# Interleaving upper-weight and lower-weight matmul passes, and moving the upper weights in SBUF, in a windowed-attention and SoLU kernel

## The chip, the cores and the metric

The kernel runs on one core of a Trainium2 chip. The metric is device time in microseconds, from the start to the end of one execution. Before the change three runs took 518.44, 518.72 and 519.62 us; their median is 518.72.

## What is computed

Attention with a causal window of 64 keys over 8 sequences of 576 tokens with 8 heads of 64, and behind it a gated projection block on the 4608 resulting rows of 512:

```python
scores = scale * np.matmul(q, k.transpose(0, 1, 3, 2))
mask = (rel >= 0) & (rel < window)
attn = softmax(np.where(mask, scores, -1e9))
x = np.matmul(attn, v)                      # rows of 512
h = x @ w_in                                # 512 -> 1024
solu = h * softmax(h)
ln = (solu - mean(solu)) / np.sqrt(var(solu) + 1e-06) * g_ln
out = ln @ w_out                            # 1024 -> 512
```

All of it is in float32, and most of the multiplications belong to the two projections.

## The kernel before, in words

The 4608 rows are 36 tiles of 128. For each tile there are scores, a softmax, a transposition of its weights, the products with v, the input projection (`moe_in`), the SoLU and its normalisation, another transposition, and the output projection (`moe_out`). The tiles are staggered: while tile t is in `moe_in`, tile t - 2 is in `moe_out`.

**The passes.** TensorE runs a float32 matmul at half rate, in two instructions. So from input tile 3 (`PLAIN_IN`) and output tile 2 (`PLAIN_OUT`) on, each operand is held as an upper part, rounded to the float32r format, and a lower part, the remainder in the same format; upper times upper, upper times lower and lower times upper are added up in PSUM. One such product of a 128x128 stationary operand and a 128x512 moving one is called a pass here. The stationary operand is a column block of x or y (`xH`, `xL`, `yH`, `yL`), the moving one a row of weights of 512 float32r values, 2048 bytes in each partition: `WH`, the upper weights, in the two const tiles `w_inH` and `w_outH`, or `WL`, the lower weights, in tiles of the ring `w`. `split` (line 384) makes both from the weights that `weight_block` decoded, with the normalisation's gain `g_sb` multiplied into the output's.

A tile's input projection has 24 passes (L601): for each of four blocks c of x, two halves d of 512 columns, and three products. The halves lie in two PSUM banks (`pH`). A tile's output projection also has 24 (L735): eight blocks f of y and three products, taken in pairs f, f + 1, all into one bank (`pO`). In both, one loop writes out six passes at a time, in the order of the list `passes` (lines 594 and 730): upper x with upper weights twice, lower x with upper weights twice, upper x with lower weights twice. Input tile 3 alone is done in two halves, its passes sorted so that all with upper weights come first (line 597). In the last tiles `moe_out` places the transposition of the next tile's halves between its passes (`middle`, line 732).

**The order.** `Plan` collects every operation with its engine, a planner's cost (a pass: 235) and what it reads and writes. TensorE's operations keep the order in which the program names them; the other engines' are placed by due times that follow from TensorE's order, with hand-set offsets (`HINTS`). SyncE's queue issues all DMAs.

**The places.** Tiles of the pool `const` come first in SBUF, in the order of their making, each padded to a multiple of 32 bytes in a partition; then the rings. Between `w_inH` and the ring of q and k lie 2 x 16384 bytes of weights, 32 of `g_sb` and 32 for `neghalf`; the ring of q and k has 3 x 5120, and every ring behind it that a pass reads starts a multiple of 2048 bytes further on. By 2048 bytes, `w_inH` and `w_outH` begin at a rest of 896, and `w`, `xH`, `xL`, `yH` and `yL` at 1984 (896 + 64 + 15360 = 7 x 2048 + 1984). Each slice of weights that a pass reads is 2048 bytes long and has its tile's rest; the blocks of x and y are 512 bytes apart.

Of the kernel before, what the change touches and what calls it, by code (L numbers as in the profile page):

```python
# [9 lines left out]
F32 = mybir.dt.float32  # L10
# [9 lines left out]
P = 128  # L20
# [206 lines left out]
def tile_window_attention_solu_moe(  # L227
# [25 lines left out]
    NC = DM // P  # L253
    NF = DFF // P
# [4 lines left out]
    const = ctx.enter_context(tc.tile_pool(name="const", bufs=1))  # L259
# [20 lines left out]
    for first in (0, None, 1):  # L280
# [3 lines left out]
        if first is not None:  # L284
            nc.gpsimd.memset(t[first * WIN:(first + 1) * WIN, :WIN], NEG)

    w_inH = const.tile([P, NC, DFF], F32R, name="w_inH")
    w_outH = const.tile([P, NF, DM], F32R, name="w_outH")
    g_sb = const.tile([P, NF], F32, name="g_sb")
    neghalf = const.tile([P, 1], F32, name="neghalf")  # L290
    nc.gpsimd.memset(neghalf, -0.5)

# [2 lines left out]
    def T(tag, n, shape, dtype=F32, pool=None):  # L295

        if (tag, n) not in plan.tiles:
            plan.tiles[tag, n] = (pool or sb).tile(
                shape, dtype, tag=tag, name=f"{tag}_{n}", bufs=RINGS[tag])
        return plan.tiles[tag, n]  # L300
# [8 lines left out]
    def W32(i):  # L309
        return T("w", i, [P, 2, 512])  # L310

    def WL(i):
        return T("w", NW + i, [P, 2, 512], F32R)

    def WH(i, x):
        if i < NC:
            return w_inH[:, i, x * 512:(x + 1) * 512]
        return w_outH[:, 2 * (i - NC) + x]
# [121 lines left out]
    def PE_T(t, x):  # L440
        return PS(NTILE + t)[:, x]
# [102 lines left out]
    def XH(t):  # L544
        return T("xH", t, [P, NC, P], F32 if t < PLAIN_IN else F32R)
# [31 lines left out]
    def PH(t):  # L577
        return T("pH", t, [P, DFF], pool=ps_h)

    def E(t):  # L580
        return T("e", t, [P, DFF])

    def moe_in(t, h):
        if t < PLAIN_IN:

            for c in range(NC if h == 0 else 0):
                for x in range(2):
                    plan.op("PE", 860, lambda c=c, x=x: nc.tensor.matmul(  # L588
                        PH(t)[:, x * 512:(x + 1) * 512], XH(t)[:, c], W32(c)[:, x],
                        start=(c == 0), stop=(c == NC - 1)),  # L590
                        [("xH", t, c // 2), ("w", c), ("w", c, x)], [("pH", t)])
            return
        kinds = (XH, WH, "xH", "H", 0), (XH, WL, "xH", "w", NW), (XL, WH, "xL", "H", 0)
        passes = [(c, d, *kinds[k]) for c in range(NC) for d, k in ((0, 0), (1, 0), (0, 2), (1, 2), (0, 1), (1, 1))]
        if t == PLAIN_IN:

            passes = sorted((p for p in passes if p[1] == h), key=lambda p: p[5] == "w")
        elif not h:
            passes = []
        for n, (c, d, x, w, xk, wk, o) in enumerate(passes):  # L600
            plan.op("PE", 235, lambda n=n, c=c, d=d, x=x, w=w: nc.tensor.matmul(  # L601
                PH(t)[:, d * 512:(d + 1) * 512], x(t)[:, c], WH(c, d) if w is WH else WL(c)[:, d],
                start=all(p[1] != d for p in passes[:n]), stop=all(p[1] != d for p in passes[n + 1:])),
                [(xk, t), (wk, o + c, d)], [("pH", t)])
# [37 lines left out]
    def YH(t):  # L642
        return T("yH", t, [P, NF, P], F32 if t < PLAIN_OUT else F32R)

    def YL(t):
        return T("yL", t, [P, NF, P], F32R)

    def crosses(t):
        return CROSS_FROM <= t < NTILE - CROSS_END
# [21 lines left out]
    def moe_join(t):  # L671
        def Y(h):
            return T("y", t, [P, NF, P])[:, 4 * h:4 * h + 4]

        for h in range(2):
            hs = slice(4 * h, 4 * h + 4)
            plan.op("DVE", 740, lambda h=h: nc.vector.tensor_copy(
                Y(h).bitcast(U16).rearrange("p f (n w) -> p f w n", w=2),
                TP(t, h).rearrange("p w f n -> p f w n")),
                [("raw", NW + 2 * t + 1, 2 + h)], [("y", t, h)], port=True)  # L680
            plan.op("ACT", 620, lambda h=h, hs=hs: nc.scalar.copy(YH(t)[:, hs], Y(h)),
                    [("y", t, h)], [("yH", t, h)])
            plan.op("DVE", 690, lambda h=h, hs=hs: nc.vector.tensor_sub(
                YL(t)[:, hs], Y(h), YH(t)[:, hs].bitcast(F32)),
                [("y", t, h), ("yH", t, h)], [("yL", t, h)], port=True)

    def moe_transpose(t, halves=range(2)):
        if crosses(t):
            moe_join(t)
            return  # L690
        for h in halves:
            def pT(h=h):
                return PE_T(t, h)

            def emit(h=h, pT=pT):
                for f in range(4):
                    c = 4 * h + f
                    nc.tensor.transpose(pT()[:, f], E(t)[:, c * P:(c + 1) * P], ident)  # L698

            hs = slice(4 * h, 4 * h + 4)  # L700
            plan.op("PE", 430, emit, [("e", t, h)], [("pS", NTILE + t, h)])
            if t < PLAIN_OUT:
                plan.op("DVE", 690, lambda hs=hs, pT=pT: nc.vector.tensor_tensor(
                    YH(t)[:, hs], pT(), g_sb[:, hs].unsqueeze(2).to_broadcast([P, 4, P]), op=ALU.mult),
                    [("pS", NTILE + t, h), ("g",)], [("yH", t, h)])
                continue
            plan.op("ACT", 560, lambda hs=hs, pT=pT: nc.scalar.copy(YH(t)[:, hs], pT()),  # L707
                    [("pS", NTILE + t, h)], [("yH", t, h)])
            plan.op("DVE", 690, lambda hs=hs, pT=pT: nc.vector.tensor_sub(  # L709
                YL(t)[:, hs], pT(), YH(t)[:, hs].bitcast(F32)),  # L710
                [("pS", NTILE + t, h), ("yH", t, h)], [("yL", t, h)])

    def moe_out(t, middle=None):

        tag = ("pO", t)

        def PO():
            return T(*tag, [P, DM], pool=ps_o)

        if t < PLAIN_OUT:  # L720
            for f in range(NF):
                plan.op("PE", 860, lambda f=f: nc.tensor.matmul(  # L722
                    PO(), YH(t)[:, f], W32(NC + f // 2)[:, f % 2],
                    start=(f == 0), stop=(f == NF - 1)),
                    [("yH", t, f // 4), ("w", NC + f // 2), ("w", NC + f // 2, f % 2)], [tag])
        kinds = (
            (YH, lambda i, x: WH(i, x), "yH", "H", 0),
            (YH, lambda i, x: WL(i)[:, x], "yH", "w", NW),
            (YL, lambda i, x: WH(i, x), "yL", "H", 0))
        passes = [(f + d, *kinds[k]) for f in range(0, NF, 2) for d, k in ((0, 0), (1, 0), (0, 2), (1, 2), (0, 1), (1, 1))]  # L730
        for n, (f, y, w, yk, wk, o) in enumerate(passes if t >= PLAIN_OUT else []):
            if n in (NF // 2 * 3, NF // 4 * 9) and middle is not None:
                moe_transpose(middle, (f // 2 % 2,))
            i, x = NC + f // 2, f % 2
            plan.op("PE", 235, lambda n=n, f=f, i=i, x=x, y=y, w=w: nc.tensor.matmul(  # L735
                PO(), y(t)[:, f], w(i, x), start=(n == 0), stop=(n == len(passes) - 1)),
                [(yk, t, f // 4), (wk, o + i, x)], [tag])

        def ot():
            return T("ot", t, [P, DM])  # L740

        if t == NTILE - 1:
            for x, copy in enumerate((nc.scalar.copy, nc.vector.tensor_copy)):
                xs = slice(x * DM // 2, (x + 1) * DM // 2)
                plan.op("DVE" if x else "ACT", 360, lambda xs=xs, copy=copy: copy(ot()[:, xs], PO()[:, xs]),
                        [tag], [("ot", t, x)])
                plan.dma(P * DM * 2, lambda xs=xs: nc.sync.dma_start(out[t * P:(t + 1) * P, xs], ot()[:, xs]),
                         [("ot", t, x)], [], True)
            return
        plan.op("ACT", 580, lambda: nc.scalar.copy(ot(), PO()), [tag], [("ot", t)])  # L750
        plan.dma(P * DM * 4, lambda: nc.sync.dma_start(out[t * P:(t + 1) * P, :], ot()), [("ot", t)], [],
                 t > SPL, 420)
# [49 lines left out]
    for t in range(NTILE + BEHIND):  # L802
# [6 lines left out]
        if t == PLAIN_IN:  # L809
            for i in range(NC):  # L810
                split(i)
        on(moe_in, t, 0)
        if t == 0:
            scores(2)
            softmax(2)
        if t < BEHIND:
            on(moe_in, t, 1)
            on(moe_norm, t)
            on(moe_cross, t)
# [78 lines left out]
```

## Time and profile before

| | |
|---|---|
| median of three runs | 518.72 us |
| the profiled execution | 518.59 us |
| its span, first to last instruction | 516.7 us |
| TensorE busy | 497.0 us, 96% |
| VectorE busy | 409.2 us, 79% |
| ScalarE busy | 355.3 us, 69% |
| GpSimd busy | 315.2 us, 61% |
| mean granted clock of TensorE | 1.00 |

The profile is of one execution. Its times are in microseconds unless marked ns; PE is TensorE's matmuls, PEld its weight loads, DVE VectorE, ACT ScalarE, POOL GpSimd, and L601 is line 601 of the kernel. Matmuls overlap their successors, so the length of one row is longer than the distance between two starts, and the pace is read from the starts.

### The profile page before, as it was taken

The numbers are of one execution on the slowest core, as the hardware profiler recorded it, in microseconds if no ns is written. First come the engines' busy times: TensorE is split into PE (matmuls) and PEld (weight loads), VectorE is DVE, ScalarE is ACT, GpSimd is POOL, SyncE is SP. The second block draws the span as 40 slices with busy tenths as digits, with TensorE's granted clock in tenths as the row PEclk, the third lists the DMA queues.
The fourth block names the chain that finished last, engine by engine and source line by source line (L and its number), as shares of the span: only waits on it lengthen the run. The fifth ranks groups of instructions, "written<-read, shape, count | busy, mean of one in ns | idle before, by whom it ended". The sixth has DMA issues, their size and how long they took to land.

```text
span 516.7 us, 11600 instructions
## 1 busy us (share of the span) xinstructions
PE 497.0 (96%) x4064; PEld 391.7 (76%) x4064; DVE 409.2 (79%) x1176; ACT 355.3 (69%) x960; POOL 315.2 (61%) x566
## 2 busy tenths in 40 slices
PE   2789999999999999999999999999999999999997
PEld 1445567888888888787888888888888888888875
DVE  5998997878887879796978798877888878877531
ACT  4589795867686858586867777675858585855331
POOL 4388566665757575747474857484747476945430
PEclk9999999999999999999999999999999999999999
DMA  8994455977999989878888897879797968654301
GB/s 322 412 410 161 122 119 127 217 159 153 209 185 173 202 203 185 200 186 187 198 167 212 162 226 165 225 151 236 127 253 145 246 120 224 124 123 102 82 20 43
DMA packets 150762, 94.09 MB, mean 182 GB/s; under 512 B 135088, under 2 KB 135344, under 8 KB 150320
## 3 DMA queue, kind: packets, MB, share of 16 engines
q1 hardware_dynamic: 150704, 93.35, 75.6%
q8 instruction: 32, 0.52, 0.5%
q14 instruction: 26, 0.21, 0.1%
HBM read 50.86 MB, written 9.44 MB: 117 GB/s over the span
## 4 chain that ended last, share of the span: by engine, by line
PE 89%; POOL 2%; ACT 1%; DVE 1%; issue 0%; ACTq 0%
PE pO L735 37%; PE pH L601 35%; PE pO L557 7%; PE pS L458 6%; PE pO L722 3%; PE pH L588 1%; POOL sS L496 1%; PE pS L698 1%; ACT sS L478 0%; POOL mst L624 0%; DVE w L391 0%; DVE yL L709 0%; POOL raw L358 0%; ACT sq L627 0%; ACT yH L707 0%; DVE e L621 0%
## 5 line engine op out<-in xcount | busy, mean ns | idle before, releaser
L496 POOL TENSOR_SCALAR sS<-sS,rec 128x128 f32<-128x128 f32 x280 | 147.9, 550 | 11.7 <-PE pS L458 7.4
L478 ACT ACTIVATE sS<-sS,nmx 128x128 f32<-128x128 f32 x288 | 111.5, 389 | 1.5 <-DVE nmx L473 1.4
L735 PE MATMUL pO<-w_outH,yH 128*128 128x512 f32 x272 | 86.9, 400 | 0.0
L735 PE MATMUL pO<-w_outH,yL 128*128 128x512 f32 x272 | 85.4, 394 | 0.0
L735 PE MATMUL pO<-w,yH 128*128 128x512 f32 x272 | 84.8, 393 | 0.0
L601 PE MATMUL pH<-w_inH,xL 128*128 128x512 f32 x264 | 83.5, 394 | 0.0
L601 PE MATMUL pH<-w_inH,xH 128*128 128x512 f32 x264 | 83.5, 395 | 0.0
L601 PE MATMUL pH<-w,xH 128*128 128x512 f32 x264 | 81.9, 393 | 0.0
L510 ACT COPY raw<-sS 128x1024 uint16<-128x1024 uint16 x64 | 66.7, 1046 | 20.9 <-POOL sS L496 20.9
L630 POOL TENSOR_SCALAR mst<-mst 128x1 f32<-128x1 f32 x36 | 21.4, 593 | 79.4 <-ACT sq L627 42.8
L638 POOL TENSOR_SCALAR e<-e,mst 128x512 f32<-128x512 f32 x72 | 66.8, 938 | 3.8
L571 ACT CAST xH<-pO 128x512 fp32r<-128x512 f32 x33 | 19.4, 586 | 71.1 <-PE pO L557 71.1
L616 DVE TENSOR_REDUCE mst<-pH 128x1 f32<-128x1024 f32 x36 | 44.0, 1222 | 30.2 <-PE pH L601 30.1
L520 DVE COPY PT<-raw 128x1024 uint16<-128x1024 uint16 x64 | 50.2, 792 | 19.9 <-DMA raw<-raw 19.6
L735 PEld LDWEIGHTS pO<-w,yH 128*128 128x128 f32 x272 | 50.9, 187 | 12.4
L735 PEld LDWEIGHTS pO<-w_outH,yL 128*128 128x128 f32 x272 | 51.1, 188 | 11.7
L624 POOL TENSOR_SCALAR mst<-mst 128x1 f32<-128x1 f32 x36 | 18.8, 523 | 66.7 <-DVE mst L621 60.7
L735 PEld LDWEIGHTS pO<-w_outH,yH 128*128 128x128 f32 x272 | 49.5, 188 | 12.7 <-issue 2.6
L601 PEld LDWEIGHTS pH<-w_inH,xH 128*128 128x128 f32 x264 | 49.6, 188 | 12.0 <-DVE mst L625 0.2
L601 PEld LDWEIGHTS pH<-w,xH 128*128 128x128 f32 x264 | 49.4, 187 | 12.0
L601 PEld LDWEIGHTS pH<-w_inH,xL 128*128 128x128 f32 x264 | 49.6, 188 | 11.3 <-issue 0.2
L627 ACT ACTIVATE sq<-e,mst 128x1024 bf16<-128x1024 f32 x36 | 41.4, 1150 | 20.0 <-POOL mst L624 20.0
(71 smaller groups left out, 850.3 us busy)
## 6 DMA issues: line engine op xcount, KB each, us to landing
qk<-qk SPq DMA_DIRECT2D x36, 640.0 KB, 5.9
v<-vS SPq DMA_DIRECT2D x36, 512.0 KB, 4.6
y<-ot SPq DMA_DIRECT2D x35, 256.0 KB, 2.5
raw<-w_out SPq DMA_DIRECT2D x4, 1024.0 KB, 11.9
raw<-w_in SPq DMA_DIRECT2D x3, 1024.0 KB, 11.7
raw<-raw SPq DMA_TRANSPOSE x126, 3.2
raw<-w_in SPq DMA_DIRECT2D x2, 512.0 KB, 6.2
y<-ot SPq DMA_DIRECT2D x2, 128.0 KB, 1.7
```

The lines of the kernel that those rows point to most:

```text
L458: nc.tensor.matmul(PS(t, p // 2)[half * WIN:(half + 1) * WIN, r, p], q[rs, p, half * WIN:(half + 1) * WIN], keys, start=True, stop=True)
L478: plan.op("ACT", 390, lambda h=h: nc.scalar.activation(SS(t)[:, h], SS(t)[:, h], AF.Exp, bias=cols("nmx", h), scale=-1.0, accum_out=cols(" ...
L496: plan.op(engine, cost, lambda h=h: v.tensor_scalar(SS(t)[:, h], SS(t)[:, h], rec()[:, h:h + 1], 0.0, ALU.mult, ALU.add), [R], [("sS", t, ...
L510: plan.op("ACT", 1050, lambda x=x: nc.scalar.copy(XP(t)[:, x], SS(t)[:, 4 * x:4 * x + 4].bitcast(U16).rearrange("p h (n w) -> p w (h n)", ...
L520: plan.op("DVE", 740, lambda x=x: nc.vector.tensor_copy(PT(t)[:, 4 * x:4 * x + 4].bitcast(U16).rearrange("p h (n w) -> p h w n", w=2), XP( ...
L557: nc.tensor.matmul(PX(t, p)[r * D:(r + 1) * D, p, ks], V(t, half)[:, h * D:(h + 1) * D], PT(t)[:, h, ks], start=True, stop=True)
L601: plan.op("PE", 235, lambda n=n, c=c, d=d, x=x, w=w: nc.tensor.matmul(PH(t)[:, d * 512:(d + 1) * 512], x(t)[:, c], WH(c, d) if w is WH els ...
L616: plan.op("DVE", 1225, lambda: nc.vector.tensor_reduce(nmax(), PH(t), axis=AX.X, op=ALU.max, negate=True), [("pH", t)], [key(0)])
L627: plan.op("ACT", 1150, lambda: nc.scalar.activation(T("sq", t, [P, DFF], BF16), E(t), AF.Square, bias=nmean(), scale=1.0, accum_out=ss()), ...
L630: plan.op("POOL", 240, lambda: nc.gpsimd.tensor_scalar(kk(), ss(), se(), se(), ALU.mult, ALU.mult), [key(1), key(3)], [key(5)])
L638: plan.op("POOL", 770, lambda h=h, hs=hs: nc.gpsimd.tensor_scalar(E(t)[:, hs], E(t)[:, hs], nmean(), kk(), ALU.add, ALU.mult), [key(4), ke ...
L735: plan.op("PE", 235, lambda n=n, f=f, i=i, x=x, y=y, w=w: nc.tensor.matmul(PO(), y(t)[:, f], w(i, x), start=(n == 0), stop=(n == len(passe ...
```

## The change

The list of six passes gets another order in both projections: upper x with upper weights and then with lower weights, the same for the second half (or block), and then lower x with upper weights twice. Two const tiles that nothing reads or writes are put in, of 272 x 4 = 1088 bytes ahead of `w_inH` and of 240 x 4 = 960 behind `g_sb`. The upper weights and `g_sb` so begin 1088 bytes later, at a rest of 1984 by 2048 bytes, and all that follows begins 2048 bytes later, at the rest that it had. The block that `middle` transposes is found from n instead of f, since f runs in another order.

```diff
+    const.tile([P, 272], F32, name="shift")
     w_inH = const.tile([P, NC, DFF], F32R, name="w_inH")
     w_outH = const.tile([P, NF, DM], F32R, name="w_outH")
     g_sb = const.tile([P, NF], F32, name="g_sb")
+    const.tile([P, 240], F32, name="gap")
     neghalf = const.tile([P, 1], F32, name="neghalf")
...
         kinds = (XH, WH, "xH", "H", 0), (XH, WL, "xH", "w", NW), (XL, WH, "xL", "H", 0)
-        passes = [(c, d, *kinds[k]) for c in range(NC) for d, k in ((0, 0), (1, 0), (0, 2), (1, 2), (0, 1), (1, 1))]
+        passes = [(c, d, *kinds[k]) for c in range(NC) for d, k in ((0, 0), (0, 1), (1, 0), (1, 1), (0, 2), (1, 2))]
...
-        passes = [(f + d, *kinds[k]) for f in range(0, NF, 2) for d, k in ((0, 0), (1, 0), (0, 2), (1, 2), (0, 1), (1, 1))]
+        passes = [(f + d, *kinds[k]) for f in range(0, NF, 2) for d, k in ((0, 0), (0, 1), (1, 0), (1, 1), (0, 2), (1, 2))]
         for n, (f, y, w, yk, wk, o) in enumerate(passes if t >= PLAIN_OUT else []):
             if n in (NF // 2 * 3, NF // 4 * 9) and middle is not None:
-                moe_transpose(middle, (f // 2 % 2,))
+                moe_transpose(middle, (n // 6 % 2,))
```

## Rows read from the trace of the kernel before

**Rows 1.** The page: busy time, share and count; the chain's shares by line.
```profile
PE 497.0 (96%) x4064; PEld 391.7 (76%) x4064; DVE 409.2 (79%) x1176; ACT 355.3 (69%) x960; POOL 315.2 (61%) x566
...
PE pO L735 37%; PE pH L601 35%; PE pO L557 7%; PE pS L458 6%; PE pO L722 3%; PE pH L588 1%; POOL sS L496 1%; PE pS L698 1%; ACT sS L478 0%; POOL mst L624 0%; DVE w L391 0%; DVE yL L709 0%; POOL raw L358 0%; ACT sq L627 0%; ACT yH L707 0%; DVE e L621 0%
```

**Rows 2.** The page's costliest groups: two of the six groups of passes.
```profile
L735 PE MATMUL pO<-w_outH,yH 128*128 128x512 f32 x272 | 86.9, 400 | 0.0
...
L601 PE MATMUL pH<-w_inH,xL 128*128 128x512 f32 x264 | 83.5, 394 | 0.0
```

**Rows 3.** Waits of TensorE, the first of eight: us in total, times, longest.
```profile
PE pS L531 <- DVE sS L496: 4.9, 1, 4.9
...
```

**Rows 4.** 100 to 480 us: busy PE, PEld, DVE, ACT, POOL (counts), granted clock, DMA share, GB/s.
```profile
100.00:480.00 380.00, 380.00 (x3185) 311.51 (x3184) 310.32 (x894) 270.41 (x728) 246.18 (x433) 1.00 0.83 181
```

**Rows 5.** The longest wait of any engine in the same stretch.
```profile
ACT xH L571 <- PE pO L557: 64.2, 15, 4.9
...
```

**Rows 6.** The chain in order of time: start, us, what.
```profile
202.53 5.55 PE pH L601 x24
208.07 5.55 PE pO L735 x24
```

**Rows 7.** Timeline of TensorE, input tile 13: start, us, pass, count.
```profile
202.36 0.62 PE L601 MATMUL pH<-w_inH,xH 128*128 128x512 f32 x2
202.82 0.63 PE L601 MATMUL pH<-w_inH,xL 128*128 128x512 f32 x2
203.29 0.62 PE L601 MATMUL pH<-w,xH 128*128 128x512 f32 x2
203.75 0.62 PE L601 MATMUL pH<-w_inH,xH 128*128 128x512 f32 x2
204.21 0.63 PE L601 MATMUL pH<-w_inH,xL 128*128 128x512 f32 x2
204.68 0.62 PE L601 MATMUL pH<-w,xH 128*128 128x512 f32 x2
205.14 0.62 PE L601 MATMUL pH<-w_inH,xH 128*128 128x512 f32 x2
205.59 0.63 PE L601 MATMUL pH<-w_inH,xL 128*128 128x512 f32 x2
206.06 0.62 PE L601 MATMUL pH<-w,xH 128*128 128x512 f32 x2
206.52 0.62 PE L601 MATMUL pH<-w_inH,xH 128*128 128x512 f32 x2
206.98 0.63 PE L601 MATMUL pH<-w_inH,xL 128*128 128x512 f32 x2
207.45 0.62 PE L601 MATMUL pH<-w,xH 128*128 128x512 f32 x2
207.91 0.39 PE L735 MATMUL pO<-w_outH,yH 128*128 128x512 f32 x1
```

**Rows 8.** The view of the tile w_outH: first pass, last writing of the lower weights.
```profile
L735 PE MATMUL pO<-w_outH,yH x272: 391/392/502, 90.1 to 511.7; 128*128 128x512 f32 x136
...
L397 DVE SCALAR_TENSOR_TENSOR w<-w,g_sb,w_outH x8: 699/742/848, 68.3 to 83.0; 128x512 fp32r<-128x512 f32 x8
```

**Rows 9.** Timeline of TensorE, input tile 3: ends of its runs.
```profile
64.51 0.40 PE L601 MATMUL pH<-w_inH,xL 128*128 128x512 f32 x1
...
66.15 1.09 PE L601 MATMUL pH<-w,xH 128*128 128x512 f32 x4
67.08 0.39 PE L601 MATMUL pH<-w_inH,xH 128*128 128x512 f32 x1
...
68.94 1.08 PE L601 MATMUL pH<-w,xH 128*128 128x512 f32 x4
69.86 0.38 PE L698 MATMUL pS<-ident,e 128*128 128x128 f32 x2
```

**Rows 10.** The chain in order of time: an output tile in fp32.
```profile
73.01 7.06 PE pO L722 x16
```

## Prediction, made before the change was timed

> **What bounds the kernel now.** I read the page first. TensorE is busy for 497.0 us of a span of 516.7, 96%, and the lines of the two projections, L735 and L601, have 37% and 35% of the chain that ended last [rows 1]. The groups of the page say what these are: six groups of 264 or 272 matmuls of 128x512, together 3 x 264 + 3 x 272 = 1608 passes [rows 2]. Then the waits. Of TensorE's own there are eight kinds; the longest is 4.9 us, at a transposition of the start, and none is at the lines of the passes [rows 3]. In the stretch from 100 to 480 us TensorE is busy for all 380 us, at a granted clock of 1.00 (the upper of its two levels, 2.4 GHz), while VectorE has 310 us of work, ScalarE 270 and GpSimd 246 [rows 4]; the longest wait there is ScalarE's, 64.2 us, and it is for TensorE [rows 5]. So the end is set by how fast the passes follow one another, and little else.
>
> How fast they do is seen in the chain in order of time: a tile's 24 passes are one piece of 5.55 us in either projection [rows 6]. 5.55 us / 24 = 231.25 ns a pass. That is the number that this change can move: 1608 passes x 1 ns = 1.6 us, 0.3% of the whole.
>
> The pace is not one number, and the timeline of TensorE by passes shows it [rows 7]. It merges each pair of the old order. The start of a pair to the start of the next, summed over the four sixes of tile 13: upper weights with the upper x, 0.46 + 0.46 + 0.45 + 0.46 = 1.83 us for eight passes, 228.8 ns each; upper weights with the lower x, 4 x 0.47 = 1.88 us, 235 ns; lower weights, 4 x 0.46 = 1.84 us, 230 ns (each sum good to about 0.01 us, so 1 ns a pass). The moving operands of the first two pairs have the same addresses, the loads are equally large, and nothing waits. So more than its addresses decides how long a pass takes: what came before it has a part.
>
> **The change, part by part.** No instruction comes or goes. Two const tiles are reserved and never written; they shift addresses only. The edit in `moe_transpose`'s argument picks the same halves: at n = 12 the old form gives f = 4, 4 // 2 % 2 = 0, the new 12 // 6 % 2 = 0, and at n = 18 both give 1. It costs nothing. Tile 3's input passes are sorted, and come out in the old order.
>
> *The order and the other engines.* The lower x and the lower y are wanted two passes later in each six, the lower weights three (or two) passes earlier, some 0.5 to 0.7 us. All have cover: TensorE never waits at a pass, so neither lower x nor lower y is late today, and both are wanted later still [rows 3]; the lower output weights' last writing begins at 83.0 us and lasts at most 0.85, while the first pass that reads upper output weights starts at 90.1 [rows 8]. Without that cover the loss would be those 0.7 us, once. The queues are untouched: no DMA is added, and none is moved in the program; the planner may place a VectorE or ScalarE operation differently, which costs nothing while TensorE waits for nobody. A faster TensorE would need the others to follow: at 310 us of 380 VectorE has a margin of 18%, and the change can ask 1 or 2% of it.
>
> *The order and TensorE.* A pass takes its stationary operand new each time already, as many weight loads as matmuls [rows 1], so that one x now serves four passes in a row saves no load. Both projections take 5.55 us for 24 passes, though the input's alternates between two PSUM banks and the output's stays in one [rows 6]; the new order of banks (0 0 1 1 0 1) should cost nothing.
>
> *The addresses.* Upper weights begin at a rest of 896 by 2048 bytes now, everything else that a pass reads (lower weights, x and y, upper and lower) at 1984. The new place gives all of them 1984. Nothing in the trace has all operands at one rest in a long run, so this term is bounded by the nearest rows. Unfavourable end: what passes do that read one rest without a break. Tile 3 has such runs of upper weights, seven passes from 64.51 to 66.15 us and eight from 67.08 to 68.94 [rows 9]: 1.64 + 1.86 = 3.50 us for 15, 233.3 ns; the slowest pair is 235. Favourable end: the fastest pair, 228.8 ns; and since that is an average over a pair in a pattern that was not made for it, I let the low end go as far below it again as it lies below the mean, 226.3 ns. Further out, the half-rate passes of the fp32 tiles (16 in 7.06 us [rows 10], 441 ns) say that a full-rate pass without any excess would take at most half, 221 ns; nothing speaks for going there.
>
> I take the fastest pair. Reasons: the four lower-weight passes that close tile 3 (0.92 us, 230 ns) and tile 13's lower pairs (230) read everything at 1984 and are under the mean, though a change of rest comes right before or behind them; and the slow pairs, 235, are those where upper weights at 896 have settled. Sum: (228.8 - 231.25) x 1608 = -3.9 us. The profiled execution took 518.59 us (its span 516.7 and 1.9 around it), 0.13 less than the median of 518.72; so 514.7.
>
> **The rivals.**
>
> *It settles slow (slower).* The mechanism: the length of a pass depends on how the read of the moving operand falls against the load of the next stationary one, and runs of one rest lock into the long position, as tile 3's 15 passes with upper weights did at 233.3 ns [rows 9]. Today the jump from 896 to 1984 and the one back, in every six passes, break that lock, and make the 228.8 that follow them; with one rest no jump is left. Price: (233.3 - 231.25) x 1608 = +3.3 us, 522.0; at the 235 of the slowest pair +6.0. It decides if the mean of the new passes is over 231.9 ns. For it: it is the only long run in the trace whose moving operands share one rest. Against it: that run's stationary operands had another rest than its moving one, as the new passes don't have.
>
> *Addresses change nothing (same).* TensorE reads both operands, and if the two reads don't hinder each other, or if only the mean counts, one order is as good as another: tile 3's eight lower-weight passes took 0.93 + 0.92 = 1.85 us, 231.3 ns, with all at 1984 [rows 9], exactly today's mean. Then 518.6 to 518.8. The Trainium skill speaks for this one (TensorE: Matmul & The Clock Gate, Part 2): the moving operand and the weight load have SBUF read ports of their own, and loading the next weights takes nothing from the running matmul. By that rule no shift of addresses could pay. The trace disagrees in part: equal passes differ by 228.8 to 235 ns [rows 7].
>
> *The change doesn't do what it says.* If rests by 2048 are not what counts, only the order is left: four changes between upper and lower weights in six passes instead of two. This falls into one of the two cases above, and has no chance of its own.
>
> **How the numbers follow.** A measurement of this kernel can tell about 0.2%, 1.0 us or 0.65 ns a pass, from no change. Forecast 0.50 (nearly all of it faster), slow settling 0.30, nothing changes 0.20. That gives faster 0.49, same 0.20, slower 0.31. The range: below, 226.3 ns, -8.0 us, 510.7; above, the slow settling at 522.0 and some 0.4 for a schedule that the planner makes worse, 522.4. About 1 in 10 is left out on either side, 235 ns for all passes above, and anything near 221 ns below. Signs are mixed, so the forecast's own range: 510.7 to 517.5.
>
> **What would show it.** Right: pieces of 24 passes at 5.49 us or less instead of 5.55, with TensorE busy throughout from 100 to 480 us still. Tile 3 keeps its order, so its 15 passes with upper weights show the address by itself: under 233 ns if one rest is the better one. Settling slow shows as pieces of 5.60. If the pieces are shorter and the total is not, waits of TensorE at L601 or L735 appear, on a VectorE subtraction or a DMA. Wrong altogether: pieces of 5.55 us as before, or pairs that differ as before though every operand has one rest.

## The result, and the profile after

The changed kernel takes 512.75 us (median of four runs, 511.89 to 513.02), the kernel before beside it 518.64 (518.44 to 519.62): ratio 0.9879, interval 0.9866 to 0.9891, 5.9 us or 1.2% faster. The forecast was 514.7: right side, inside its range, and 2 us too timid. The profiled execution took 513.01 us, with a span of 510.9. Lines behind the two new tiles have moved by two: L601 and L735 are L603 and L737 now.

The page after, busy time and the chain's shares, answers to [rows 1]:

```profile
PE 492.1 (96%) x4064; PEld 392.4 (77%) x4064; DVE 409.8 (80%) x1176; ACT 355.6 (70%) x960; POOL 314.5 (62%) x566
...
PE pH L603 34%; PE pO L737 34%; PE pO L559 6%; PE pS L460 6%; PE pO L724 3%; PE pH L590 1%; DMA raw<-raw 1%; ACT sS L480 1%; POOL sS L498 1%; PE pS L700 1%; DVE e L623 1%; DVE mst L618 1%; DMA y<-ot 1%; ACT e L620 0%; DVE w L368 0%
```

As many instructions as before on every engine, TensorE still at 96%, and the two projections still the chain, now with 34% each instead of 35 and 37. New among the chain's shares are a few per cent of other engines; they lie ahead of one late wait, read below.

The chain in order of time (start, us, what), for [rows 6]:

```profile
195.87 5.67 PE pO L737 x24
201.54 5.44 PE pH L603 x24
206.98 5.44 PE pO L737 x24
```

A tile's piece went from 5.55 to 5.44 us, 226.7 ns a pass, in both projections. The 5.67 is a tile that follows attention; before, these took 5.76.

TensorE's timeline of the same input tile 13 as in [rows 7], start, duration, pass, count:

```profile
201.38 0.39 PE L603 MATMUL pH<-w_inH,xH 128*128 128x512 f32 x1
201.60 0.39 PE L603 MATMUL pH<-w,xH 128*128 128x512 f32 x1
201.83 0.39 PE L603 MATMUL pH<-w_inH,xH 128*128 128x512 f32 x1
...
202.74 0.39 PE L603 MATMUL pH<-w_inH,xH 128*128 128x512 f32 x1
...
206.81 0.39 PE L737 MATMUL pO<-w_outH,yH 128*128 128x512 f32 x1
```

Read starts, not durations (0.39 us overlaps the next pass). Start to start it is 0.22 or 0.23 throughout, six passes from 201.38 to 202.74 make 1.36 us, and 24 make 5.43 (5.440 by the trace's starts in ns). The unequal pairs of before are gone: upper and lower, x and weights, all pace alike.

Tile 3, whose order the change leaves alone, in the timeline after, for [rows 9]:

```profile
64.14 0.39 PE L603 MATMUL pH<-w_inH,xL 128*128 128x512 f32 x1
...
65.75 1.08 PE L603 MATMUL pH<-w,xH 128*128 128x512 f32 x4
66.67 0.39 PE L603 MATMUL pH<-w_inH,xH 128*128 128x512 f32 x1
...
68.48 1.07 PE L603 MATMUL pH<-w,xH 128*128 128x512 f32 x4
69.39 0.60 PE L700 MATMUL pS<-ident,e 128*128 128x128 f32 x4
```

Its 15 passes with upper weights take 1.61 + 1.81 = 3.42 us where they took 3.50: 228.0 ns instead of 233.3, the last eight 226 to 227. Here nothing but the address of the weights has changed.

Of the waits of TensorE after, for [rows 3], the one that is new (us in total, times, longest), and the stretch from 100 to 480 us, for [rows 4]:

```profile
PE pH L603 <- DVE mst L623: 0.8, 1, 0.8
```

```profile
100.00:480.00 380.00, 379.23 (x3233) 315.34 (x3232) 315.51 (x899) 271.54 (x728) 246.03 (x432) 1.00 0.84 182
```

48 more of TensorE's instructions (3233 for 3185) fit into the same 380 us, at the same granted clock of 1.00. VectorE has 315.5 us of work in it instead of 310.3. And TensorE is no longer busy for all of it: 0.77 us are idle, one wait at a pass (L603), where before there was none.

**Where the time went.** I compared the start of each of the 67 tiles in the two timelines. Of a tile that follows another without a break, 46 in all, the step to the next start is 0.107 us shorter; of the 19 that begin behind attention or other work it is about 0.094, since their first passes don't pace yet (below), and of the two with a transposition between their passes 0.055. That makes 46 x 0.107 + 19 x 0.094 + 2 x 0.055 = 6.8 us. In the trace the lead over the kernel before grows from 0.38 us at tile 3 to 1.14 at output tile 5, and falls to 0.32 at input tile 8, where the wait is: against the step that was due, 0.93 us go in the wait and 0.08 at the tile's first pass, and the others run at 227 ns at once. Another 0.27 us goes at input tile 12, 0.15 in a short wait and 0.12 in nine passes that fall into step again. Then the lead grows without a break to 5.76 at the last output tile; the span is 516.7 - 510.9 = 5.8 us shorter. So the gain is the passes' pace, less 1.3 us that two late releases of one buffer took back. The 0.38 us at the start varies with the run: the same kernel once more (e8) begins tile 3 only 0.07 us earlier than before, e1 0.18 later.

**The new wait.** The chain in order of time names its steps, last ones here (start, us, what):

```profile
131.55 1.21 ACT e L620 x2
...
132.78 1.22 DVE e L623
...
134.16 5.68 PE pH L603 x24
```

Tile 8's first pass writes the PSUM buffer pH, and must wait until VectorE (L623) has read the earlier tile there; VectorE waited for ScalarE's e (L620). The chain puts a transfer ahead of L620, but ScalarE was not idle before it, so that isn't what it waited for. ScalarE's own timeline (start, us, operation, in brackets the idle time before it and what ended it) shows what L620 stood behind, after and, at the same place, before:

```profile
128.73 1.05 ACT L512 COPY raw<-sS 128x1024 uint16<-128x1024 uint16 x1 [1.09 <-POOL sS L498]
130.59 1.05 ACT L512 COPY raw<-sS 128x1024 uint16<-128x1024 uint16 x1 [0.82 <-POOL sS L498]
131.55 1.11 ACT L620 ACTIVATE e<-pH,mst 128x1024 f32<-128x1024 f32 x1
```

```profile
129.19 1.05 ACT L510 COPY raw<-sS 128x1024 uint16<-128x1024 uint16 x1 [1.09 <-POOL sS L496]
130.59 1.05 ACT L510 COPY raw<-sS 128x1024 uint16<-128x1024 uint16 x1 [0.35 <-POOL sS L496]
131.54 1.11 ACT L618 ACTIVATE e<-pH,mst 128x1024 f32<-128x1024 f32 x1
```

L620 is queued behind a copy of attention scores, and that copy waits for GpSimd's scaling (L498). The first copy came 0.46 us earlier than before, as TensorE's lead there would have it; the second came at 130.59 in both. So e began when it had before, while TensorE came for the buffer sooner. Before, the same buffer was free 0.5 us ahead of its use: that was the slack, and the faster passes used it up.

Why GpSimd's second batch was no earlier, VectorE's timeline shows, after and, at the same place, before:

```profile
129.16 0.85 DVE L679 COPY y<-raw 128x1024 uint16<-128x1024 uint16 x1
```

```profile
129.13 1.23 DVE L616 TENSOR_REDUCE mst<-pH 128x1 f32<-128x1024 f32 x1 [0.56 <-PE pH L601]
130.27 1.73 DVE L677 COPY y<-raw 128x1024 uint16<-128x1024 uint16 x2
```

Before, VectorE stood 0.56 us waiting for TensorE at L616, and its copy began only at 130.27; the four scalings of GpSimd's second batch took 0.38 us each. After, TensorE was ahead, that wait was gone, the copy ran from 129.16 to 130.01, and the scaling that began inside it, at 129.37, took 0.84 us. The rest of the trace before agrees: the 14 scalings with VectorE's copy L664 alone beside them took 0.80 to 1.38 us, the 95 with its L616 or L621 beside them, and the 23 with nothing, 0.36 to 0.38. So the faster passes moved a VectorE operation, and that one lengthened GpSimd's; by what means, no row shows.

### The profile page after: what moved, and what is told of

Its sections match the earlier page's. It is cut to its first block, busy times and chain, and to the rows that moved or that the text cites. A ratio compares the mean times of both kernels' runs of the same rounds, so it can differ in the third digit from the quotient of the medians.

```text
span 510.9 us, 11601 instructions
## 1 busy us (share of the span) xinstructions
PE 492.1 (96%) x4064; PEld 392.4 (77%) x4064; DVE 409.8 (80%) x1176; ACT 355.6 (70%) x960; POOL 314.5 (62%) x566
## 4 chain that ended last, share of the span: by engine, by line
PE 85%; DVE 4%; ACT 2%; POOL 2%; DMA 2%; issue 0%; SPq 0%; ACTq 0%; DVEq 0%; POOLq 0%
PE pH L603 34%; PE pO L737 34%; PE pO L559 6%; PE pS L460 6%; PE pO L724 3%; PE pH L590 1%; DMA raw<-raw 1%; ACT sS L480 1%; POOL sS L498 1%; PE pS L700 1%; DVE e L623 1%; DVE mst L618 1%; DMA y<-ot 1%; ACT e L620 0%; DVE w L368 0%
## 5 line engine op out<-in xcount | busy, mean ns | idle before, releaser
L498 POOL TENSOR_SCALAR sS<-sS,rec 128x128 f32<-128x128 f32 x280 | 149.2, 554 | 10.8 <-PE pS L460 7.4
L737 PE MATMUL pO<-w_outH,yH 128*128 128x512 f32 x272 | 108.2, 398 | 0.0
L737 PE MATMUL pO<-w,yH 128*128 128x512 f32 x272 | 106.1, 390 | 0.0
L603 PE MATMUL pH<-w_inH,xH 128*128 128x512 f32 x264 | 103.7, 393 | 0.8 <-DVE mst L623 0.8
L603 PE MATMUL pH<-w,xH 128*128 128x512 f32 x264 | 101.8, 389 | 0.0
L737 PE MATMUL pO<-w_outH,yL 128*128 128x512 f32 x272 | 83.9, 389 | 0.0
L603 PE MATMUL pH<-w_inH,xL 128*128 128x512 f32 x264 | 81.9, 389 | 0.0
L632 POOL TENSOR_SCALAR mst<-mst 128x1 f32<-128x1 f32 x36 | 19.9, 553 | 79.8 <-ACT sq L629 42.9
L737 PEld LDWEIGHTS pO<-w_outH,yH 128*128 128x128 f32 x272 | 51.0, 188 | 12.7 <-issue 2.6
L737 PEld LDWEIGHTS pO<-w_outH,yL 128*128 128x128 f32 x272 | 51.1, 188 | 10.9
L603 PEld LDWEIGHTS pH<-w_inH,xH 128*128 128x128 f32 x264 | 49.6, 188 | 12.2 <-PE pO L737 1.2
L737 PEld LDWEIGHTS pO<-w,yH 128*128 128x128 f32 x272 | 51.1, 188 | 10.0
L603 PEld LDWEIGHTS pH<-w_inH,xL 128*128 128x128 f32 x264 | 49.6, 188 | 10.6 <-issue 0.2
L603 PEld LDWEIGHTS pH<-w,xH 128*128 128x128 f32 x264 | 49.6, 188 | 10.4 <-issue 0.2
L626 POOL TENSOR_SCALAR mst<-mst 128x1 f32<-128x1 f32 x36 | 18.9, 524 | 62.3 <-DVE mst L623 56.5
```

The costliest lines, as they stand in the source:

```text
L498: plan.op(engine, cost, lambda h=h: v.tensor_scalar(SS(t)[:, h], SS(t)[:, h], rec()[:, h:h + 1], 0.0, ALU.mult, ALU.add), [R], [("sS", t, ...
L632: plan.op("POOL", 240, lambda: nc.gpsimd.tensor_scalar(kk(), ss(), se(), se(), ALU.mult, ALU.mult), [key(1), key(3)], [key(5)])
```

## The experiments

Two theories stood after the result. By the **distance**: what counts is how far the moving operand's start lies from the stationary operand's start, modulo some number of bytes, and distance 0 is the good one. By the **moving operand's own place**: what counts is where the weights lie by themselves. Against both stood the part that needs no address: the new order of the passes. In the kernel before, all but the upper weights begin at a rest of 1984 by 2048; the upper weights, at 896, are 1984 - 896 = 1088 bytes short of it.

### e1_move_only: the tiles moved, the old order

```diff
-        passes = [(c, d, *kinds[k]) for c in range(NC) for d, k in ((0, 0), (0, 1), (1, 0), (1, 1), (0, 2), (1, 2))]
+        passes = [(c, d, *kinds[k]) for c in range(NC) for d, k in ((0, 0), (1, 0), (0, 2), (1, 2), (0, 1), (1, 1))]
...
-        passes = [(f + d, *kinds[k]) for f in range(0, NF, 2) for d, k in ((0, 0), (0, 1), (1, 0), (1, 1), (0, 2), (1, 2))]
+        passes = [(f + d, *kinds[k]) for f in range(0, NF, 2) for d, k in ((0, 0), (1, 0), (0, 2), (1, 2), (0, 1), (1, 1))]
```

> The upper weights moved as in the change, the order of the passes as before. Theory D (distance): a pass's length follows from how far the rest of its moving operand is from the rest of the stationary operand that is loaded meanwhile, and with one rest for all it settles at 226.7 ns in any order; so pieces of 24 passes of 5.44 us and about 512.7 us, 1.2% under the kernel before. Theory O (order): the interleaving is needed to get there; then the pieces stay above 5.49 us and half of the gain or more is missing, 515.5 to 518.6 us. If the one wait of 0.8 us at input tile 8 comes from the faster passes it is here too; if it comes from the new order of the list it is gone and the time is some 0.9 us lower.

Measured: 512.98 us (511.86 to 513.64), ratio 0.9885 (0.9871 to 0.99). The chain in order of time:

```profile
253.13 5.44 PE pH L603 x24
258.57 5.44 PE pO L737 x24
```

The move alone gives the whole gain, with the pace of the change. With all operands at one rest the order is worth nothing that these runs can tell. The wait at tile 8 is not here; there is a shorter one, 0.2 us, at input tile 12, and another in attention (read under e8), so the time is no lower.

### e2_order_only: the new order, the tiles not moved

```diff
-    const.tile([P, 272], F32, name="shift")
...
-    const.tile([P, 240], F32, name="gap")
```

> The new order of the passes, the upper weights where they were, at a rest of 896. Theory D: the distance changes four times in six passes instead of twice, no pass settles, pieces of 24 stay between 5.49 and 5.65 us, time 516 to 522 us. Theory O: pieces of 5.44 us and about 512.7 us.

Measured: 515.60 us (515.3 to 515.95), ratio 0.9937 (0.9921 to 0.9954). The chain, and TensorE's timeline of input tile 13:

```profile
253.99 5.49 PE pH L601 x24
```

```profile
201.56 0.39 PE L601 MATMUL pH<-w_inH,xH 128*128 128x512 f32 x1
...
202.93 0.39 PE L601 MATMUL pH<-w_inH,xH 128*128 128x512 f32 x1
```

Six passes take 1.37 us, 228.9 ns by the finer starts, against 231.1 in the old order: 1608 x 2.2 = 3.5 us, and 518.76 - 515.60 = 3.2 were measured. So where the rests differ, the order does count, and by itself gives half of the gain. The two parts of the change do not add up: after the move nothing is left for the order to give. The piece lies on the edge of what the expectation gave the theory of the distance, the time 0.4 us outside: it named no pace for mixed distances, and the runs give no rule for one.

### e3_move64: the upper weights moved by 64 bytes only

```diff
-    const.tile([P, 272], F32, name="shift")
+    const.tile([P, 16], F32, name="shift")
...
-    const.tile([P, 240], F32, name="gap")
+    const.tile([P, 496], F32, name="gap")
```

> The change with the upper weights moved by 64 bytes instead of 1088, to a rest of 960; that is the rest of the others by 1024, 512, 256 and 128 bytes, but not by 2048. If only a short period of the addresses counts (the blocks of x are 512 bytes apart and no pass before showed it), 5.44 us a piece and 512.7 us, as with the change. If the rest by 2048 counts, pieces above 5.49 us and 515.5 us or more.

Measured: 513.12 us (512.35 to 514.68), ratio 0.9894 (0.9875 to 0.9913). The chain:

```profile
252.34 5.44 PE pH L603 x24
```

Upper weights at 960 instead of 1984 pace just as well. They need not share the other operands' rest by 2048; 1984 - 960 = 1024 bytes of distance is as good as none. The period that counts is 1024 or a part of it, and the old distance, 1088, was 64 off.

### e4_offsets: the stationary operands moved instead

The weights stay where the change has them. The buffers of x and y get longer rows and a pad, so that the stationary operands lie 0 (x of even tiles), 64 (x, odd), 32 (y, even) and 128 bytes (y, odd) beyond a multiple of 512 from the moving ones. All four distances are in one run, one tile of each in every four.

```diff
+    def pad(tag, n):
+        if n and ("pad", tag) not in plan.tiles:
+            plan.tiles["pad", tag] = sb.tile([P, n // 4], F32, tag="pad" + tag, name="pad" + tag, bufs=1)
...
-        return T("xH", t, [P, NC, P], F32 if t < PLAIN_IN else F32R)
+        pad("xH", 0)
+        return T("xH", t, [P, NC * P + 16], F32 if t < PLAIN_IN else F32R)[:, :NC * P].rearrange("p (c n) -> p c n", c=NC)
...
+        pad("xL", 352)
+        return T("xL", t, [P, NC * P + 112], F32R)[:, :NC * P].rearrange("p (c n) -> p c n", c=NC)
...
+        pad("yH", 416)
+        return T("yH", t, [P, NF * P + 24], F32 if t < PLAIN_OUT else F32R)[:, :NF * P].rearrange("p (c n) -> p c n", c=NF)
...
+        pad("yL", 96)
+        return T("yL", t, [P, NF * P + 24], F32R)[:, :NF * P].rearrange("p (c n) -> p c n", c=NF)
```

> The change, with the stationary operands put at four places: even input tiles at the common rest (distance 0), odd input tiles 64 bytes further, even output tiles 32 bytes further, odd output tiles 128 bytes further (by 512 bytes); all moving operands stay at one rest. Theory D: even input tiles 5.44 us; odd input tiles settle as the upper weights did alone in input tile 3 before the change, 233.3 ns a pass, 5.60 us; the other two tell the dependence. Rival theory M: it is the moving operand's own place that counts, 1984 being a good one and 896 a bad one, and the stationary one's place does nothing; then all four kinds of tile stay at 5.44 us.

Measured: 519.1 us, one run. The chain, distances 32, 64, 128 and 0 in this order (the first tile follows attention):

```profile
249.45 5.79 PE pO L745 x24
255.24 5.60 PE pH L609 x24
260.83 5.58 PE pO L745 x24
266.41 5.44 PE pH L609 x24
```

TensorE's timeline has six passes of the tile at 64 and of the one at 0 side by side:

```profile
255.07 0.40 PE L609 MATMUL pH<-w_inH,xH 128*128 128x512 f32 x1
...
256.47 0.40 PE L609 MATMUL pH<-w_inH,xH 128*128 128x512 f32 x1
...
266.25 0.39 PE L609 MATMUL pH<-w_inH,xH 128*128 128x512 f32 x1
...
267.61 0.39 PE L609 MATMUL pH<-w_inH,xH 128*128 128x512 f32 x1
```

1.40 us against 1.36, 233.3 ns against 226.7: the same weights at the same place, the same order, the same kernel, and only x 64 bytes further. The moving operand's own place falls as the sole cause; the distance stands. And 233.3 at distance 64 is what tile 3's upper passes took in the kernel before [rows 9], at 1088 = 4 x 256 + 64.

Two things this leaves open. No run moves both operands together: in all of them the good place of either is 192 by 256 bytes (1984 = 7 x 256 + 192), so a rule in which each operand has to be at 192 by itself fits too. For the distance speaks that the same 64 bytes gave the same 233.3 ns and the same steps of 236 and 231 in turn, once with the weights off that place and x on it (the first half of tile 3 before), once the other way round (here). And all stationary operands of a tile share one rest, so the runs can't tell whether the pass's own stationary operand counts or the one that is loaded meanwhile.

### e5_offsets, e6_offsets and e7_fine: the period and its shape

The edit of e4 with other numbers: 256 (x even), 384 (x odd), 192 (y even) and 448 (y odd) in e5; 480, 320, 96 and 288 in e6. The lower parts xL and yL are moved alike; their lines are left out below.

```diff
+        pad("xH", 256)
+        return T("xH", t, [P, NC * P + 32], F32 if t < PLAIN_IN else F32R)[:, :NC * P].rearrange("p (c n) -> p c n", c=NC)
...
+        pad("yH", 192)
+        return T("yH", t, [P, NF * P + 64], F32 if t < PLAIN_OUT else F32R)[:, :NF * P].rearrange("p (c n) -> p c n", c=NF)
```

```diff
+        pad("xH", 480)
+        return T("xH", t, [P, NC * P + 88], F32 if t < PLAIN_IN else F32R)[:, :NC * P].rearrange("p (c n) -> p c n", c=NC)
...
+        pad("yH", 448)
+        return T("yH", t, [P, NF * P + 48], F32 if t < PLAIN_OUT else F32R)[:, :NF * P].rearrange("p (c n) -> p c n", c=NF)
```

In e7 the operands lie 16 (x even), 240 (x odd), 208 (y even) and 176 bytes (y odd) into longer rows.

```diff
+        o = (16, 240)[t % 2] // 4
+        return T("xH", t, [P, NC * P + 64], F32 if t < PLAIN_IN else F32R)[:, o:o + NC * P].rearrange("p (c n) -> p c n", c=NC)
...
+        o = (208, 176)[t % 2] // 4
+        return T("yH", t, [P, NF * P + 64], F32 if t < PLAIN_OUT else F32R)[:, o:o + NF * P].rearrange("p (c n) -> p c n", c=NF)
```

> As the four places before, other distances by 512 bytes: even input tiles 256, odd input tiles 384, even output tiles 192, odd output tiles 448 bytes. Theory D with a period of 512: only distance 0 is at 226.7 ns, or a new distance shows a better place; with a period of 256: even input tiles at 256 take 5.44 us as at 0, and 448 (192 by 256) as even output tiles at 192; with a period of 128 nothing could differ from 0 and 64, which the 128 of the run before contradicts already (about 232 ns). Theory M: 5.44 us everywhere, contradicted as well.

> Distances 480 (even input tiles), 320 (odd input tiles), 96 (even output tiles) and 288 (odd output tiles). Theory D with a period of 256: 320 behaves as 64 (233.3 ns, 5.60 us), 288 as 32, 480 as 224. With a period of 512 they need not. A place better than distance 0 would show as a piece under 5.44 us, and would be the version that beats the change.

> Finer distances, by 256 bytes (the period that the two runs before showed): even input tiles 16, odd input tiles 240, even output tiles 208, odd output tiles 176 bytes. If the pace changes by steps of 64 bytes, 240 and 208 behave as 192 (228.9 ns, 5.49 us) and 16 as 0 (226.7); if every few bytes count, they lie between their neighbours or above both: 233 for 16 and 240 (32 and 224 took 233.3), 229 to 233 for 208, 229 to 233 for 176. A piece under 5.44 us would be a better place than the change's.

Measured, one run each: 516.33, 522.04 and 518.57 us. In all three the first tile shown follows attention. The chain of e5, distances 192, 384, 448, 256 in this order:

```profile
248.44 5.71 PE pO L745 x24
254.14 5.58 PE pH L609 x24
259.72 5.50 PE pO L745 x24
265.22 5.46 PE pH L609 x24
```

Of e6, distances 96, 320, 288, 480:

```profile
250.57 5.81 PE pO L745 x24
256.38 5.60 PE pH L609 x24
261.98 5.60 PE pO L745 x24
267.58 5.59 PE pH L609 x24
```

Of e7, distances 208, 240, 176, 16:

```profile
249.49 5.77 PE pO L741 x24
255.25 5.49 PE pH L605 x24
260.74 5.53 PE pO L741 x24
266.27 5.59 PE pH L605 x24
```

The starts in the timelines, once a tile has settled, give ns a pass by distance (modulo 256):

```
distance    0      16     32     64     96     128          176    192    208    224    240
ns a pass   226.7  233.3  233.3  233.3  234.3  232.4        230.0  228.9  231.8  233.3  228.3
again +256  226.7         233.3  233.3         232.4               228.9
```

The five distances tried twice, 256 apart, agree to 0.1 ns (128 on output tiles and 384 on input tiles among them), so at these the pace repeats every 256 bytes. It does not repeat sooner: a shorter period that divides 256 would divide 128 too, and 128 is not like 0. Zero is the best of the eleven, and sharp: 16 bytes beyond it cost 6.6 ns, 16 short of it 1.6. Steps of 64 bytes are out: 16 is not like 0, nor 208 like 192. The 233 expected for 240 was a miss, and no place better than 0 was found. e6, with all its tiles at 233 or 234 ns, is what the prediction's slow rival would have been: 522.04 us, for the 522.0 worked out then.

### e8_again: the change once more, for the wait

```diff
+
+# the change once more
```

> The changed kernel once more, unaltered, for the one wait of 0.8 us at input tile 8 that its first profile shows. If the faster passes or the planner's order cause it, it is there again, at the same tile and of about the same length; if it is a matter of when a transfer lands, it is gone or at another tile, and the span is up to 0.9 us shorter than the 510.9 us of the first profile.

Measured: 513.39 us. TensorE's one wait at a pass is 1.1 us long. The chain ahead of it:

```profile
167.17 8.63 DMA raw<-raw
...
181.06 1.94 POOL sS L498 x4
...
183.03 1.01 ACT raw L512
...
185.21 1.23 DVE e L623
```

The same kernel now goes through tile 8 unhindered and waits at input tile 12. The last steps are those of the wait at tile 8: GpSimd's scaling of scores, the copy on ScalarE behind it, e, VectorE's reading of pH. What is at their head differs: here a transposing transfer of 8.6 us that VectorE's queue stood behind. Its span, 511.2 us, is not shorter than the first, as the expectation had it for a wait that goes away. The same wait stands in e1 at input tile 12, 0.2 us long. There is a second kind of wait: e1 and e3 lose 0.9 and 0.7 us ahead of output tile 26, where attention's products with v wait for VectorE's copy of the transposed weights (wait of TensorE in e3: us in total, times, longest):

```profile
PE pO L559 <- DVE PT L522: 0.3, 1, 0.3
```

In e1 and e3 the transposing transfer before that copy took 4.9 us, and VectorE stood 2.4 us waiting for it. So the wait for pH came in three of the four traces with the good pace, at tile 8 or 12, and not in the trace before; which link is late varies with the run. Taking it away was not tried.

## Why the prediction was right, and where it was off

**What bounds it.** Right. The passes set the end, and the time moved with their pace: 231.1 ns to 226.7 by starts, 4.45 ns, x 1608 = 7.2 us; less 19 x 0.013 us for the tiles behind other work, 0.1 at the two with a transposition inside and 1.3 us at two late releases, and with the 0.38 us by which tile 3 began earlier, that makes 5.9, for 5.8 in the spans.

**The term that was mis-sized.** The prediction took "the fastest pair, 228.8 ns" as the new pace. It is 226.7. The pair's 228.8 was an average in a mixture: the kernel before never held one distance long enough to settle but in tile 3. The reasons for taking it were weaker than they looked. By the trace's starts in ns the three kinds of pair in tile 13 take 229.1, 233.3 and 230.9 ns a pass; the rows, to 0.01 us, made 228.8, 235 and 230 of them. So the lower pairs, which "read everything at 1984", were not "under the mean" of 231.1 by anything that counts, and tile 3's eight such passes, too few to settle, took 231.3. The choice of the favourable end was right, and luck had a part in it. The low end, 226.3, put as far below the fastest pair as that is below the mean, was nearly right, for no reason that was known then. From 226.7 the sum would have given 1608 x 4.55 = 7.3 us and 511.3, and the 1.7 us from there to the profiled 513.01 is mostly the 1.3 us at the two late releases; waits at a pass the prediction named as a sign to look for, and put at nothing in its sum.

**The order, put at nothing.** Right for the change as a whole, and wrong as a general statement: with unequal rests the order alone was worth 3.2 us (e2).

**Everything at one rest by 2048.** The right place for a reason wider than given. As far as the runs can tell (e4), it is the distance to the stationary operand that counts, with a period of 256 bytes at the distances tried twice; a move by 64 does as much as the move by 1088 (e3). In the kernel before, the passes with lower weights had distance 0 and those with upper weights 64, modulo 256, and their mixture made the unequal pairs of [rows 7].

**The cover.** Lower weights, lower x and y never made TensorE wait at a pass, as forecast. That "a faster TensorE would need the others to follow", with VectorE's margin of 18%, was read from the wrong quantity: the busy share says that the others can keep up on average, and they do. The release of pH is a chain through the queues of GpSimd, ScalarE and VectorE, and its slack was 0.5 us at tile 8. 0.8 to 1.4 us were lost to late work of the other engines in each of the four runs traced with the good pace, at that buffer or, in e3, in attention.

**The rivals.** *It settles slow*: its mechanism is real, passes do lock into 233.3 ns when the distance is wrong (e4, e6), and [rows 9] showed just that. But the prediction's objection to it, that tile 3's operands had different rests, was the point that decided. *Addresses change nothing*: out. The weights stayed put in e4, x moved by 64 bytes, and a pass went from 226.7 to 233.3 ns. The Trainium skill's sentence that loading the next weights takes no read bandwidth from the running matmul (TensorE: Matmul & The Clock Gate, Part 2) is no ground here for leaving addresses out: the pace of these passes depends on how the two operands' addresses lie to each other. That the two reads hinder one another would fit, but no run shows the reads themselves. *The change doesn't do what it says* had no chance of its own. Its condition came true, rests by 2048 are not what counts (e3); what it drew from that did not, since the move alone is the gain (e1).

**What would show it.** Two signs of being right came: pieces under 5.49 us, and tile 3 under 233 ns. The third, TensorE busy throughout from 100 to 480 us, did not: 0.77 us were idle. The wait at L603 was on VectorE, but not on a subtraction: it was on L623, which reads the earlier tile out of pH.

No version among the runs beats the change: e1 and e3 have intervals that overlap its own.

## What to carry to other kernels

Where passes with a weight load each bound a float32r kernel, put the start of every moving operand at the same rest by 256 bytes as the start of its stationary one; a pad tile of some bytes does it, and here it was worth 1.2%. Both rests were 192 here; another common one, other types and other shapes were not tried. Read the pace from start to start in a long run of equal passes: a single pair, or the mean of a mixed pattern, tells neither the best nor the worst. Before counting on a faster engine, look for the smallest slack at a buffer's release, not at the busy share of the others.

## What the runs showed of the hardware that was not expected

- The pace is a lock, not an average: at distance 0 all settled passes follow at 226 or 227 ns, upper and lower alike, and 5.440 us for 24 is 226.67 ns, 544 cycles at the granted 2.4 GHz. At a wrong distance the starts go through a fixed pattern, in e4 at distance 64 alternately 236 and 231 ns, in e6 at 320 steps of 233 and 234 with the same mean.
- It takes up to ten passes to lock. In most of the changed kernel's output tiles behind attention the starts are 337, 231, 231, 236, 228, 232 and 231 ns apart, and then 227; in tiles 3 and 4, behind the fp32 tiles, it takes ten; behind the wait at tile 8, one.
- The dependence on the distance is not smooth: 228.3 ns at 240, 233.3 at 224, 231.8 at 208, 228.9 at 192. Nothing in the runs says why.
- A GpSimd scaling of 128x128 took 0.36 to 0.38 us beside VectorE's L616 or L621, and 0.80 to 1.38 beside its copy L664, in the trace before.
- 226.7 is not the 215.7 ns from start to start that the Trainium skill gives for back-to-back matmuls of 512 columns at the upper clock (TensorE: Matmul & The Clock Gate, "Wait — 56ns, not 53.3ns?"). No run here settled below 226.7, though single steps of 224 to 226 ns occur in mixed patterns; what holds the passes there, with a new stationary operand each, stays open.
